# Streamed weights copied into contiguous blocks, with a ring of three double pieces in place of five single ones

## Chip, cores, metric

The kernel runs on one core of a Trainium2 chip. The metric is device microseconds of one execution. Each experiment was timed against the kernel before on the same chip, in turns. Medians are quoted, and ratios with 95% intervals.

## The reference, cut to what matters

Four residual layers, A, B, A, B, work on a sequence of 2048 rows of width 640. Layer A is recurrent. It cuts the sequence into segments, and the first 8 rows of the attention's input (the memory) come from the result of the segment before.

```python
for s in range(n_seg):
    xs = x[:, s * seg_len:(s + 1) * seg_len, :].copy()     # seg_len = 32
    h = jnp.concatenate([mem, xs], axis=1)                 # 8 + 32 rows of 640
    q = jnp.einsum('btd,dhe->bhte', h, Wq)                 # 32 heads of 192
    k = jnp.einsum('btd,dhe->bhte', h, Wk)
    v = jnp.einsum('btd,dhe->bhte', h, Wv)
    ...                                                    # masked softmax attention
    o = jnp.einsum('bhte,hed->btd', o, Wo)
    mem = o[:, :M, :].copy()                               # M = 8: needed by the next segment
    outs.append(o[:, M:, :])
```

The 64 segments of a layer A cannot run side by side, so a segment's latency is paid 64 times per layer and 128 times in all.

## The kernel before

Wk, Wq and Wv are each 640 x 6144 in bfloat16. They are viewed as 128 partitions x 5 row groups `b` x 6144 columns, and the columns are worked in four head groups `r` of 1536. Of the 60 pieces (3 weights, 4 `r`, 5 `b`) those with `b` of 0 to 2 stay in SBUF. The other 24 pieces, of 384 KB each, are streamed from DRAM again in every segment, through a ring of five. A piece has 3072 bytes per partition, and its rows are 61440 bytes apart in DRAM.

```python
def pieces(pool, m, r, nb=5):
    out = []
    for b in range(KC):
        if (m, r, b) in streamed:                      # b = 3, 4
            t = pool.tile([P, PW], BF16, name="wring", tag="wring", bufs=nb)
            nc.sync.dma_start(out=t[:], in_=wview[m][:, b, PW * r:PW * r + PW])
            out.append(t)
        else:
            out.append(res[m, r, b])
    return out
...
for s in range(NSEG):
    load_rows(xrs[s % 2], x_dram, s)                   # 4 small loads on SP's queue
    if s + 1 < NSEG:
        load_rows(hxs[(s + 1) % 2], xn_dram, s + 1)    # 4 more
    ...
    for r in range(NR):
        for m in "KQV":
            w = pieces(sp, m, r)
            for b in range(KC):
                for g in range(4):
                    nc.tensor.matmul(ps[32 * g:32 * g + 32, 0:384], lhsT=hT[:, b, :], rhs=rhs, ...)
            # K, Q: raw (ACT), then transposes to KT, QT (DVE); V: Vp (ACT, DVE)
        # scores S from KT and QT (PE); E = exp(S) (ACT); normalised to Pt; O = Pt Vp (PE); OT; W += OT Wo
    ...
    hT = hx_transpose(s + 1)                           # then its memory columns, from W: next segment
```

In the timelines below PE keeps to its queue's order: a matmul whose operand is not there holds what stands behind it.

The softmax here doesn't subtract the row's maximum and nothing guards it: scores larger than these inputs give would overflow.

Of the kernel before, what the change touches and what calls it, by code (L numbers as in the profile page):

```python
# [8 lines left out]
P = 128  # L9
BF16 = mybir.dt.bfloat16  # L10
# [88 lines left out]
class Kernel:  # L99
# [130 lines left out]
    def build_A_consts(self):  # L230
# [19 lines left out]
            nc.vector.memset(ones[32 * g:32 * g + 32, 32 * g:32 * g + 32], 1.0)  # L250
        self.ones_blk = ones

    def layer_A(self, x_dram, xn_dram, xout_dram, li):
        nc, tc = self.nc, self.tc
        KC, NSEG = self.KC, self.NSEG
        dram = self.dram
        NR = 4
        PW = 1536
        self.kqb_d = dram.tile([NSEG, P, NR, 224], BF16, name=f"kqb{li}")
        self.vb_d = dram.tile([NSEG * 8, NR, 4, 512], BF16, name=f"vb{li}")  # L260
        self.otb_d = dram.tile([NSEG, P, 384], BF16, name=f"otb{li}")
        wsrc = {"K": self.A_Wk, "Q": self.A_Wq, "V": self.A_Wv}
        wview = {m: w.rearrange("(p b) h d -> p b (h d)", b=KC) for m, w in wsrc.items()}
        streamed = {(m, r, b) for m in "KQV" for r in range(NR) for b in (3, 4)}
        with tc.tile_pool(name=f"A{li}_wres", bufs=1) as wres:
            res = {}
# [3 lines that stand above are left out]
                        if (m, r, b) not in streamed:  # L270
                            t = wres.tile([P, PW], BF16, name=f"w{m}{r}{b}")
                            nc.sync.dma_start(out=t[:], in_=wview[m][:, b, PW * r:PW * r + PW])
                            res[m, r, b] = t
            wo = wres.tile([P, 48, 640], BF16, name="wo_res")

            def pieces(pool, m, r, nb=5):
                out = []
                for b in range(KC):
                    if (m, r, b) in streamed:
                        t = pool.tile([P, PW], BF16, name="wring", tag="wring", bufs=nb)  # L280
                        nc.sync.dma_start(out=t[:], in_=wview[m][:, b, PW * r:PW * r + PW])
                        out.append(t)
                    else:
                        out.append(res[m, r, b])
                return out

            self.A_pre(xn_dram, li, pieces)
            for r in range(NR):
                nc.sync.dma_start(out=wo[:, 12 * r:12 * r + 12, :], in_=self.A_Wo.rearrange("h d m -> (h d) m").rearrange(
                    "(c p) m -> p c m", p=P)[:, 12 * r:12 * r + 12, :])  # L290
            self.A_chain(x_dram, xn_dram, xout_dram, li, pieces, wo)
            self.A_post(x_dram, xout_dram, li, wo)

    def A_pre(self, xn_dram, li, pieces):
        nc, tc, ev, KC, NSEG = self.nc, self.tc, self.ev, self.KC, self.NSEG
        NR = 4
        NT = NSEG // 16
        TP = P // NSEG
        with tc.tile_pool(name=f"A{li}_pre", bufs=1) as pp, \
                tc.tile_pool(name=f"A{li}_preps", bufs=8, space=bass.MemoryType.PSUM) as ps_:  # L300
            xv = xn_dram.rearrange("(s t) d -> t s d", t=32)
            xBT = pp.tile([P, KC, 8 * NSEG], BF16, name="xBT")
            for k in range(NT):
                xb = pp.tile([P, 640], BF16, name="xB", tag="xB", bufs=1)
                for t2 in range(TP):
                    nc.gpsimd.dma_start(out=xb[NSEG * t2:NSEG * t2 + NSEG, :], in_=xv[24 + TP * k + t2])
                pt = ps_.tile([P, 1024], BF16, name="pt", tag="bank")
                for b in range(KC):
                    self.transp(out=pt[:, P * b:P * b + P], in_=xb[:, :].rearrange("p (q b) -> p b q", b=KC)[:, b, :],
                                identity=self.ident[:, :])  # L310
                for t2 in range(TP):
                    t = TP * k + t2
                    ev.copy(out=xBT[:, :, :].rearrange("p b (s t) -> p b s t", t=8)[:, :, :, t],
                            in_=pt[:, 0:640].rearrange("p (b q) -> p b q", b=KC)[:, :, NSEG * t2:NSEG * t2 + NSEG])
            stage = [pp.tile([P, 16, 224], BF16, name=f"stage{i}") for i in range(2)]
            vst = [pp.tile([P, 4, 512], BF16, name=f"vst{i}") for i in range(1)]
            for t in stage:
                nc.vector.memset(t[:], 0.0)
            for t in vst:
                nc.vector.memset(t[:], 0.0)  # L320
            n = 0
            for r in range(NR):
                wk = pieces(pp, "K", r, 4)
                wq = pieces(pp, "Q", r, 4)
                for tb in range(NT):
                    st = stage[n % 2]
                    n += 1
                    for m, w in (("K", wk), ("Q", wq)):
                        for pi in range(4):
                            ps = ps_.tile([P, 512], F32, name="ps_pre", tag="bank")  # L330
                            for i in range(3):
                                c = 3 * pi + i
                                for b in range(KC):
                                    nc.tensor.matmul(ps[:, P * i:P * i + P], lhsT=w[b][:, P * c:P * c + P],  # L334
                                                     rhs=xBT[:, b, P * tb:P * tb + P], start=(b == 0), stop=(b == KC - 1))
                            src = ps[:, 0:384].rearrange("p (i s t) -> p i s t", i=3, t=8)
                            if m == "Q":
                                for i in range(3):
                                    o = 128 + 8 * (3 * pi + i)
                                    ev.copy(out=st[:, :, o:o + 8], in_=src[:, i])  # L340
                            else:
                                o = 32 * pi
                                ev.copy(out=st[:, :, o:o + 8], in_=src[:, 0])
                                ev.copy(out=st[0:64, :, o + 8:o + 16], in_=src[0:64, 1])
                                ev.copy(out=st[64:P, :, o + 16:o + 24], in_=src[64:P, 1])
                                ev.copy(out=st[:, :, o + 24:o + 32], in_=src[:, 2])
                    nc.gpsimd.dma_start(out=self.kqb_d[16 * tb:16 * tb + 16, :, r, :].rearrange("s p f -> p s f"), in_=st[:])
                wv = pieces(pp, "V", r, 4)
                for tb in range(NT):
                    vt = vst[0]  # L350
                    for g in range(4):
                        ps = ps_.tile([P, 512], F32, name="ps_pre", tag="bank")
                        for b in range(KC):
                            nc.tensor.matmul(ps[:, 0:384], lhsT=xBT[:, b, P * tb:P * tb + P], rhs=wv[b][:, 384 * g:384 * g + 384],
                                             start=(b == 0), stop=(b == KC - 1))
                        ev.copy(out=vt[:, g, 0:192], in_=ps[:, 0:192])
                        ev.copy(out=vt[:, g, 320:512], in_=ps[:, 192:384])
                    nc.gpsimd.dma_start(out=self.vb_d[P * tb:P * tb + P, r, :, :], in_=vt[:])

    def A_chain(self, x_dram, xn_dram, xout_dram, li, pieces, wo):  # L360
        nc, tc, KC, NSEG = self.nc, self.tc, self.KC, self.NSEG
        scale = float(self.Dh) ** -0.5
        NR = 4
        with tc.tile_pool(name=f"A{li}_ch", bufs=2) as sp, \
# [9 lines left out]
            def load_rows(dst, src, s):  # L374
                for g in range(4):
                    nc.sync.dma_start(out=dst[32 * g + 8:32 * g + 32, :], in_=src[32 * s:32 * s + 24, 160 * g:160 * g + 160])
# [11 lines left out]
            for s in range(NSEG):  # L388
                load_rows(xrs[s % 2], x_dram, s)
                if s + 1 < NSEG:  # L390
                    load_rows(hxs[(s + 1) % 2], xn_dram, s + 1)
                otb = sp.tile([P, NR, 12, 8], BF16, name="otb", tag="otb")
                kqb = vb = None
                W = pop.tile([P, 512], F32, name="ps_w", tag="w")
                for r in range(NR):
# [11 lines left out]
                    for m in "KQV":  # L407
                        w = pieces(sp, m, r)
# [9 lines left out]
                        if m == "V":  # L418
                            nc.scalar.activation(out=Vp[:, :].rearrange("p (a c) -> p a c", c=64)[:, 0:3, :],  # L419
                                                 in_=ps[:, 0:192].rearrange("p (a c) -> p a c", c=64), func=ACT.Copy)  # L420
# [71 lines left out]
                for g in range(4):  # L492
                    nc.gpsimd.dma_start(out=xout_dram[32 * s:32 * s + 24, 160 * g:160 * g + 160],  # L493
                                        in_=ob[32 * g + 8:32 * g + 32, :])
# [236 lines left out]
```

## Time and profile before

| | before |
|---|---|
| three runs: median, lowest, highest | 5964.28 us, 5961.47, 5976.45 |
| profiled span, clock granted to PE | 5972.0 us, 0.877 |
| the two recurrent chains | 2118.4 and 2125.4 us |
| mean segment | 34.22 us |
| SP's first load for the first layer norm | 55.2 us |

In the following a segment starts when the cast that completes its `hT` starts. A transfer has landed when the last of its 16 engines has reported. These numbers are worked out from the trace's records of transfers and instructions, as are all "per segment" numbers below. (The prediction's 34.07 us is the same mean over a shorter stretch.)

From the page of the kernel before, part 2: one digit for each fortieth of the span, in tenths. "PEclk" is the granted clock.

```profile
PE   1877777777777777767848777777777777777777
...
PEclk9988988988888888779979889888898888888898
DMA  5678888888888888830075888888888888887301
```

The two long plateaus, where DMA is at 8, are the two chains. PE shows 7 there: neither is saturated, so a chain of dependences decides.

From the page of before, part 3, DMA queues: number of packets, MB moved, and the time that the packets took as a share of 16 engines' span. Queue q1 carries SP's transfers, nearly all of them streamed weights.

```profile
q1 hardware_dynamic: 551376, 1319.70, 65.1%
```

From the page of before, part 4: the chain of work that ended last, as shares of the span by engine and by line.

```profile
DMA 41%; PE 37%; DVE 7%; issue 7%; ACT 5%; SPq 1%; POOL 1%; DVEq 0%; POOLq 0%; ACTq 0%
DMA wring<-in_A_Wv_dram 17%; PE ps_qkv L416 17%; DMA wring<-in_A_Wk_dram 12%; DMA wring<-in_A_Wq_dram 8%; PE ps_w L481 4%; ACT raw L424 2%; PE ps_num L539 2%; PE ps_pre L334 2%; PE ps_kv L539 2%; PE ps_bqk L539 1%; PE pp L516 1%; PE ps_o L467 1%; DMA kqb<-kqb 1%; PE ps_s L442 1%; DVE QT L426 1%
```

Streamed weights take 37% of the chain (17 + 12 + 8), and PE as much.

From the waits view of PE, before (what it waited for: us in total, number of waits, longest):

```profile
PE ps_qkv L416 <- DMA wring<-in_A_Wk_dram: 120.2, 180, 2.3
PE ps_qkv L416 <- DMA wring<-in_A_Wq_dram: 119.9, 215, 3.1
PE ps_qkv L416 <- DMA wring<-in_A_Wv_dram: 116.6, 240, 2.1
...
PE ps_w L481 <- issue: 45.0, 46, 2.4
...
PE ps_s L451 <- ACT E L450: 5.7, 26, 0.2
```

 "issue" marks a wait whose end the profile cannot explain; all such lines of this view come to 100 us.

From the timeline of SP, before, one segment's end (start, duration, engine, line, operation, count). One line can stand for several issues.

```profile
2005.47 2.21 SPq L281 DMA_DIRECT2D wring<-in_A_Wv_dram  x2
2007.73 1.92 SPq L376 DMA_DIRECT2D Xr<-in_A_x_dram  x4
2009.69 2.68 SPq L376 DMA_DIRECT2D Hx<-xn  x4
2012.50 0.83 SPq L281 DMA_DIRECT2D wring<-in_A_Wk_dram  x2
```

After V of `r` = 3, SP issues eight small row loads, and the next K stands behind them. On average V lands at 29.35 us and the last of the eight is issued at about the same moment, so the DMA queue runs empty. The gap between landings is some 2.9 us longer than usual. It is called the drain below.

From the timeline of before, one set of scores in the same chain:

```profile
2021.98 0.58 DVE L426 STREAM_TRANSPOSE QT<-raw 128x384 bf16<-128x384 bf16 x1 [1.35 <-ACT raw L424]
...
2022.62 0.25 PE L442 MATMUL ps_s<-QT,KT 128*32 128x40 bf16 x3
...
2023.16 0.22 PE L446 MATMUL ps_s<-QT,kqb 128*8 128x16 bf16 x4
...
2023.48 0.26 ACT L450 ACTIVATE E<-ps_s 128x112 bf16<-128x112 f32 x1 [1.52 <-PE ps_s L446]
```

### The profile page before, as it was taken

To read this page: it belongs to the slowest core of one execution; us is meant where nothing else is said; L and a number is where in the kernel's file an instruction comes from. 1 tells how busy PE (TensorE), PEld (TensorE's weight loads), DVE (VectorE), ACT (ScalarE), POOL (GpSimd) and SP (SyncE) were. 2 spreads that over 40 slices of the span, in tenths; PEclk is the share of its full clock that TensorE was granted. 3 is DMA by queue.
4 is the path that set the end of the run, shared out by engine and by line. 5 is a ranking of instruction groups with operands and counts; after the bars stand their busy time and mean duration, and the time that the engine had idled before them with its cause. 6 is when DMAs were issued, how large, how long until landed. Compare 5 with 4: busy or idle time off the path is not lost.

```text
span 5972.0 us, 227753 instructions
## 1 busy us (share of the span) xinstructions
PE 4427.1 (74%) x99706; PEld 2457.7 (41%) x99784; DVE 2244.9 (38%) x6994; ACT 1597.1 (27%) x4729; POOL 1529.6 (26%) x3332
## 2 busy tenths in 40 slices
PE   1877777777777777767848777777777777777777
PEld 1744444444444444333337344444444444444343
DVE  3333333333333333338444333333333333332383
ACT  1322222222222222224023222222222222222230
POOL 3122232322322322220011322322322322322100
PEclk9988988988888888779979889888898888888898
DMA  5678888888888888830075888888888888887301
GB/s 176 214 255 298 294 296 297 296 294 296 290 294 301 292 303 290 271 121 16 7 269 169 285 291 298 295 293 297 289 295 295 294 293 294 301 294 241 98 21 32
DMA packets 645399, 1470.22 MB, mean 246 GB/s; under 512 B 144160, under 2 KB 200448, under 8 KB 644400
## 3 DMA queue, kind: packets, MB, share of 16 engines
q1 hardware_dynamic: 551376, 1319.70, 65.1%
q0 software_dynamic: 91648, 135.06, 7.3%
q8 instruction: 780, 12.78, 0.8%
q14 instruction: 219, 1.79, 0.1%
q10 hardware_dynamic: 1376, 0.88, 0.1%
HBM read 1372.81 MB, written 82.35 MB: 244 GB/s over the span
## 4 chain that ended last, share of the span: by engine, by line
DMA 41%; PE 37%; DVE 7%; issue 7%; ACT 5%; SPq 1%; POOL 1%; DVEq 0%; POOLq 0%; ACTq 0%
DMA wring<-in_A_Wv_dram 17%; PE ps_qkv L416 17%; DMA wring<-in_A_Wk_dram 12%; DMA wring<-in_A_Wq_dram 8%; PE ps_w L481 4%; ACT raw L424 2%; PE ps_num L539 2%; PE ps_pre L334 2%; PE ps_kv L539 2%; PE ps_bqk L539 1%; PE pp L516 1%; PE ps_o L467 1%; DMA kqb<-kqb 1%; PE ps_s L442 1%; DVE QT L426 1%
## 5 line engine op out<-in xcount | busy, mean ns | idle before, releaser
L416 PE MATMUL ps_qkv<-wring,hT 128*32 128x384 bf16 x12288 | 1504.8, 364 | 389.5 <-DMA wring<-in_A_Wk_dram 120.2
L416 PEld LDWEIGHTS <-hT 128*32 128x32 bf16 x30720 | 959.3, 104 | 1419.4 <-issue 1054.3
L424 ACT ACTIVATE raw<-ps_qkv 128x384 bf16<-128x384 f32 x1024 | 501.9, 490 | 1742.6 <-PE ps_qkv L416 1698.4
L416 PE MATMUL ps_qkv<-wK,hT 128*32 128x384 bf16 x6144 | 707.6, 390 | 227.3 <-DVE hT L489 113.5
L416 PE MATMUL ps_qkv<-wQ,hT 128*32 128x384 bf16 x6144 | 756.8, 381 | 24.9 <-issue 17.5
L481 PE MATMUL ps_w<-wo_res,OT 128*32 128x160 bf16 x24576 | 628.3, 253 | 137.4 <-ACT OT L476 89.9
L401 POOL DMA_DIRECT2D vb<-vb x1024 | 571.3, 559 | 544.5 <-PE ps_qkv L416 231.4
L481 PEld LDWEIGHTS <-OT 128*32 128x32 bf16 x24576 | 495.7, 104 | 363.6 <-ACT OT L476 272.9
L431 DVE STREAM_TRANSPOSE KT<-raw 128x128 bf16<-128x128 bf16 x1024 | 258.5, 291 | 877.7 <-ACT raw L424 877.6
L406 POOL COPY QT<-kqb 128x96 bf16<-128x96 bf16 x512 | 135.9, 266 | 1638.2 <-PE ps_s L446 1537.8
L421 DVE CAST Vp<-ps_qkv 128x192 bf16<-128x192 f32 x512 | 183.1, 358 | 832.6 <-ACT Vp L419 832.6
L416 PE MATMUL ps_qkv<-wV,hT 128*32 128x384 bf16 x6144 | 430.9, 358 | 38.2 <-ACT raw L424 33.9
L426 DVE STREAM_TRANSPOSE QT<-raw 128x384 bf16<-128x384 bf16 x512 | 296.1, 578 | 403.4 <-ACT raw L424 397.1
L477 DVE CAST OT<-ps_o 128x240 bf16<-128x240 f32 x512 | 208.6, 407 | 575.0 <-ACT OT L476 575.0
L478 POOL COPY otb<-OT 128x96 bf16<-128x96 bf16 x512 | 139.0, 272 | 812.9 <-DVE OT L477 812.9
L476 ACT ACTIVATE OT<-ps_o 128x240 bf16<-128x240 f32 x512 | 189.5, 370 | 561.2 <-PE ps_o L471 553.7
L450 ACT ACTIVATE E<-ps_s 128x112 bf16<-128x112 f32 x512 | 134.7, 263 | 696.6 <-PE ps_s L446 696.6
L442 PE MATMUL ps_s<-QT,KT 128*32 128x40 bf16 x8192 | 206.7, 185 | 99.9 <-DVE QT L426 77.6
L493 POOL DMA_DIRECT2D xres<-ob x512 | 263.4, 523 | 50.1 <-DVE hT L489 43.9
L467 PEld LDWEIGHTS <-Vp 32*128 32x128 bf16 x8192 | 148.4, 92 | 243.2 <-issue 234.1
L442 PEld LDWEIGHTS <-KT 128*32 128x32 bf16 x8192 | 144.1, 94 | 250.0 <-DVE QT L426 228.5
L467 PE MATMUL ps_o<-Pt,Vp 32*128 32x40 bf16 x8192 | 192.0, 179 | 45.1 <-DVE Pt L460 45.0
(412 smaller groups left out, 6091.7 us busy)
## 6 DMA issues: line engine op xcount, KB each, us to landing
wring<-in_A_Wk_dram SPq DMA_DIRECT2D x1040, 384.0 KB
wring<-in_A_Wq_dram SPq DMA_DIRECT2D x1040, 384.0 KB
wring<-in_A_Wv_dram SPq DMA_DIRECT2D x1040, 384.0 KB
kqb<-stage POOLq DMA_DIRECT2D x32, 896.0 KB, 6.5
kqb<-kqb POOLq DMA_DIRECT2D x256, 112.0 KB, 5.0
vb<-vst POOLq DMA_DIRECT2D x32, 512.0 KB, 2.9
vb<-vb POOLq DMA_DIRECT2D x1024, 16.0 KB, 5.1
wo_res<-in_A_Wo_dram SPq DMA_DIRECT2D x8, 1920.0 KB
```

The lines of the kernel that those rows point to most:

```text
L401: nc.gpsimd.dma_start(out=vb[32 * g:32 * g + 8, :, :], in_=self.vb_d[8 * s:8 * s + 8, r:r + 2, g, :])
L416: nc.tensor.matmul(ps[32 * g:32 * g + 32, 0:384], lhsT=hT[:, b, :], rhs=rhs, start=(b == 0), stop=(b == KC - 1), tile_position=(0, 32 * g) ...
L424: nc.scalar.activation(out=raw[:], in_=ps[:, 0:384], func=ACT.Copy)
L426: nc.vector.transpose(out=QT[:, :, 8:40], in_=raw[:, :].rearrange("p (c j) -> p c j", j=32))
L431: nc.vector.transpose(out=kv[:, :, o, :], in_=rv[:, :, i, :])
L442: nc.tensor.matmul(S[32 * g:32 * g + 32, 40 * e:40 * e + 40], lhsT=KT[:, 4 * g + ks, :], rhs=QT[:, 3 * g + qc, :], start=False, stop=False ...
L467: nc.tensor.matmul(O[:, g, 40 * i:40 * i + 40], lhsT=Vp[32 * g:32 * g + 32, P * blk:P * blk + P], rhs=Pt[32 * g:32 * g + 32, 40 * e:40 * e ...
L476: nc.scalar.activation(out=ov[:, 0:2, :], in_=O[:, 0:2, 0:120], func=ACT.Copy)
L477: nc.vector.tensor_copy(out=ov[:, 2:4, :], in_=O[:, 2:4, 0:120])
L481: nc.tensor.matmul(W[32 * g:32 * g + 32, 0:160], lhsT=OT[:, c, 8:40], rhs=wo[:, 12 * r + c, 160 * g:160 * g + 160], start=(r == 0 and c == 0),
L493: nc.gpsimd.dma_start(out=xout_dram[32 * s:32 * s + 24, 160 * g:160 * g + 160], in_=ob[32 * g + 8:32 * g + 32, :])
L539: nc.tensor.matmul(ps[rows, n0:n0 + nn], lhsT=lhsT_fn(k), rhs=rhs_fn(k, n0, nn), **kw)
```

## The change

The intent: one transfer of 6144 bytes per partition instead of two of 3072, read from a block whose rows lie end to end, and a ring that holds six pieces instead of five. At the start twelve DRAM-to-DRAM copies lay the streamed weights out so. To make room, the tile `otb` goes from two buffers to one.

```diff
+        self.wst = {}
+        for r in range(4):
+            for m in "KQV":
+                t = self.dram.tile([P, 2, 1536], BF16, name=f"wst{m}{r}")
+                nc.sync.dma_start(out=t[:], in_=self.wview[m][:, 3:5, 1536 * r:1536 * r + 1536])
+                self.wst[m, r] = t
 ...
-            def pieces(pool, m, r, nb=5):
-                out = []
-                for b in range(KC):
-                    if (m, r, b) in streamed:
-                        t = pool.tile([P, PW], BF16, name="wring", tag="wring", bufs=nb)
-                        nc.sync.dma_start(out=t[:], in_=wview[m][:, b, PW * r:PW * r + PW])
-                        out.append(t)
-                    else:
-                        out.append(res[m, r, b])
+            def pieces(pool, m, r, nb=3):
+                t = pool.tile([P, 2, PW], BF16, name="wring", tag="wring", bufs=nb)
+                nc.sync.dma_start(out=t[:], in_=self.wst[m, r][:])
+                out = [res[m, r, b][:, :] for b in range(3)] + [t[:, 0, :], t[:, 1, :]]
                 return out
 ...    # the prologue before each chain: rings of 4 singles become rings of 2 doubles
-                otb = sp.tile([P, NR, 12, 8], BF16, name="otb", tag="otb")
+                otb = sp.tile([P, NR, 12, 8], BF16, name="otb", tag="otb", bufs=1)
```

More of the change, by code (lines that the diff above doesn't have):

```diff
@@ L251, in build_A_consts @@
         self.ones_blk = ones
+        wsrc = {"K": self.A_Wk, "Q": self.A_Wq, "V": self.A_Wv}
+        self.wview = {m: w.rearrange("(p b) h d -> p b (h d)", b=self.KC) for m, w in wsrc.items()}
+        self.wst = {}
[4 more added lines that the diff above has]
+                self.wst[m, r] = t
     def layer_A(self, x_dram, xn_dram, xout_dram, li):
@@ L261, in layer_A @@
         self.otb_d = dram.tile([NSEG, P, 384], BF16, name=f"otb{li}")
-        wsrc = {"K": self.A_Wk, "Q": self.A_Wq, "V": self.A_Wv}
-        wview = {m: w.rearrange("(p b) h d -> p b (h d)", b=KC) for m, w in wsrc.items()}
+        wview = self.wview
         streamed = {(m, r, b) for m in "KQV" for r in range(NR) for b in (3, 4)}
@@ L322, in A_pre @@
             for r in range(NR):
-                wk = pieces(pp, "K", r, 4)
-                wq = pieces(pp, "Q", r, 4)
+                wk = pieces(pp, "K", r, 2)
+                wq = pieces(pp, "Q", r, 2)
                 for tb in range(NT):
@@ L347, in A_pre @@
                     nc.gpsimd.dma_start(out=self.kqb_d[16 * tb:16 * tb + 16, :, r, :].rearrange("s p f -> p s f"), in_=st[:])
-                wv = pieces(pp, "V", r, 4)
+                wv = pieces(pp, "V", r, 2)
                 for tb in range(NT):
```

## The prediction

> **What bounds the kernel now.** The two recurrent layers take most of the span: 128 segments of 34.07 us mean (spacing of the hT casts in the trace, 0.7 to 2.3 ms). A segment streams 24 pieces of 384 KB. In the slices view DMA is 88% busy at about 295 GB/s; the chain of waits gives 37% of the span to the streamed weights, 37% to PE. In the waits view PE waits for streamed pieces 357 us in all, 2.8 us per segment: the most that streaming alone can give back directly.
>
> Issue and landing of every piece, timed against the segment's start, show three regimes:
> - At 29.2 us the last piece (V, r=3) lands. Only then is the last of eight small row loads issued (29.3 us), then the next K (29.8 us), which lands at 33.4 us: 4.2 us between landings instead of 1.25, a drain of about 2.9 us.
> - At 10 to 14 us piece 12 is issued late (11.0 us; its predecessor lands at 13.7): the DMA share dips from 0.97 to 0.72, since PE still held the slot. The ring of five is too short here.
> - After 14 us pieces land back to back, 1.25 us apart, and PE waits.
>
> **Costs.**
> Packets: one of 3072 bytes takes 121 ns at the median, 142 in the mean; 4096 bytes take 160, 5120 take 196. The slope is about 26.8 bytes per ns, the fixed part about 7 ns. So 6144 bytes should take about 235 ns rather than 2x121. That agrees in direction with the Trainium skill, "DMA: Bandwidth & Descriptors", "Why small descriptors are slow" (a fixed cost per packet); at 3 KB it is a 3% matter. The stalls (142 against 121) look proportional to bytes in other reads too (1280 bytes: 66 against 55; 768: 42 against 36), so I expect contiguity not to remove them: about 276 ns in the mean. With half the semaphore packets: an estimated 0.8 us per segment.
>
> Ring: three doubles are six pieces, one more ahead. Where PE holds the slots (10 to 14 us) DMA gets up to one piece, 1.25 us, further ahead, but a slot comes free only when both halves are used: 0.8 us.
>
> Unchanged: the drain (the eight small loads still follow V of r=3, and the last still waits for it, as the instruction order shows), PE's work, the 4.8 us from V's landing to the next hT.
>
> Added: twelve DRAM-to-DRAM copies, 9.4 MB, at the head of SP's queue, before the setup on the chain (SP does short setup copies until 55 us). At about 300 GB/s an estimated 30 us, once, nearly all exposed.
>
> **Sum.** 128 x 1.6 = 205 us less, 30 more: 5964 - 175 = about 5790 us. Range 5650 to 5880; faster by over 2% 0.67, within 2% 0.29, slower 0.04.
>
> **What would show it.** Packets of 6144 bytes near 235 ns median, 276 mean; 2.4 us between landings of doubles; segments near 32.5 us; a shallower dip at 10 to 14 us; the drain still about 3 us; PE's wait for streamed weights well below 357 us; the first ln_x load some 30 us later than 55 us.
>
> **What would make it wrong.** Contiguous blocks ending the stalls (mean near 240 ns): far faster, PE-bound, near 5600. Or transfers cut into smaller packets, or blocks whose rows collide in memory: no gain. Or PE, blocked in order on a whole double, delaying the scores behind it: the ring's gain lost, within 2%.

## More of the kernel before

The order of instructions on each engine is fixed by a scheduler when the kernel is built, and it need not be the order of the source.

Times inside a segment are means over both chains: 124 segments, or 110 in the table of landings.

PE waits 356.7 us for streamed pieces, and hardly at all (5.7 us) for the exponentials E of the scores.

The score matmuls follow the transposed Q (QT) at once and run through in about 0.75 us; E follows. No matmul on a streamed piece of V stands between them.

## The result, and the profile after

| | before | after |
|---|---|---|
| median of four runs (lowest, highest) | 5968.23 us (5961.47, 5976.45) | 5948.58 us (5945.19, 5965.11) |
| ratio, 95% interval | | 0.9972 [0.9949, 0.9995] |
| profiled span, clock | 5972.0 us, 0.877 | 5963.0 us, 0.876 |
| chains | 2118.4, 2125.4 us | 2095.7, 2105.6 us |
| mean segment | 34.22 us | 33.88 us |
| start of the first `hT` cast of the first chain | 377.49 us | 409.34 us |

A ratio is the mean time of one kernel's fast runs over that of the other's fast runs of the same rounds, so it is not quite the ratio of the medians quoted. Below, a ratio is turned into microseconds as (ratio - 1) x 5966; here that is -17 us. The change was predicted at -175 us.

From the page of after, part 2, the slices:

```profile
PE   0777777777777777767848677777777777777778
...
PEclk9989888888988888879879888888888888888898
DMA  5668888888888888840065788888888888887201
```

From part 3 of that page, the queue of the streamed weights; it has fewer packets, as intended, and a smaller share:

```profile
q1 hardware_dynamic: 330000, 1329.03, 63.0%
```

From part 4 of that page, the chain:

```profile
PE 40%; DMA 31%; issue 11%; DVE 9%; ACT 8%; POOL 1%; SPq 1%; DVEq 0%; ACTq 0%; POOLq 0%
PE ps_qkv L419 17%; DMA wring<-wstV 14%; DMA wring<-wstQ 10%; PE ps_w L484 7%; DMA wring<-wstK 3%; ACT raw L427 2%; DVE QT L429 2%; PE ps_num L542 2%; PE ps_bqk L542 2%; PE ps_kv L542 2%; ACT Vp L422 1%; PE ps_s L445 1%; PE pp L519 1%; PE ps_o L470 1%; ACT OT L479 1%
```

The streamed weights' part of the chain fell from 37% to 27%. "issue", DVE and ACT took it over: 7 + 7 + 5 became 11 + 9 + 8.

From the waits view of PE, after:

```profile
PE ps_s L454 <- ACT E L453: 143.6, 361, 0.6
...
PE ps_qkv L419 <- DMA wring<-wstQ: 73.3, 140, 1.6
PE ps_qkv L419 <- DMA wring<-wstK: 69.6, 88, 2.3
...
PE ps_w L484 <- issue: 64.6, 57, 2.7
...
PE ps_qkv L419 <- DMA wring<-wstV: 63.4, 112, 1.7
```

PE waits 206.3 us for streamed pieces, 150 us less. Yet the wait for E rose from 5.7 to 143.6 us, and the "issue" lines from 100 to 187 us in all. Some of those last up to 3.2 us, as long as waits for weights, so 206 us is the least that weights can still cost here. The wait changed its name more than it went away.

From the timeline of after, one set of scores:

```profile
2017.34 0.18 PE L445 MATMUL ps_s<-QT,KT 128*32 128x40 bf16 x1
...
2017.55 0.51 PE L419 MATMUL ps_qkv<-wring,hT 128*32 128x384 bf16 x8
...
2017.87 0.17 PE L449 MATMUL ps_s<-QT,kqb 128*8 128x16 bf16 x1
...
2017.92 0.18 PE L449 MATMUL ps_s<-QT,kqb 128*8 128x16 bf16 x3
...
2018.33 0.26 ACT L453 ACTIVATE E<-ps_s 128x112 bf16<-128x112 f32 x1
...
2018.64 0.20 PE L454 MATMUL ps_s<-E,ones_blk 128*128 128x80 bf16 x1 [0.21 <-ACT E L453]
```

Here the eight matmuls on V's double piece (L419) stand in PE's queue ahead of the last score matmuls. They cannot start before the whole double has landed, and E cannot start before them. Per segment, in us from its start:

| | V(r=2) lands | E(r=2) starts | K(r=3)'s evacuation starts | V(r=3) lands | next hT | E's start after QT's start, r = 0..3 |
|---|---|---|---|---|---|---|
| before | 21.99 | 21.86 | 25.14 | 29.35 | 34.22 | 1.23, 1.16, 1.36, 1.26 |
| after | 20.94 | 22.06 | 24.66 | 27.98 | 33.88 | 1.13, 2.05, 2.30, 1.99 |

V(r=2) lands 1.05 us earlier, but E of `r` = 2 starts 0.20 us later. And V(r=3) lands 1.37 us earlier, but the next segment starts only 0.34 us earlier.

From the timeline of SP, after, at the start:

```profile
0.75 0.70 SPq L259 DMA_DIRECT2D wstK<-in_A_Wk_dram  x1
...
18.49 2.13 SPq L259 DMA_DIRECT2D wstV<-in_A_Wv_dram  x1
20.95 4.84 SPq L187 DMA_DIRECT2D wbd<-zeros_t  x3
...
85.25 1.31 SPq L208 DMA_DIRECT2D ln_x<-in_A_x_dram  x3
```

From the same view of before:

```profile
1.34 1.34 SPq L187 DMA_DIRECT2D wbd<-zeros_t  x3
...
55.19 30.44 SPq L208 DMA_DIRECT2D ln_x<-in_A_x_dram  x16
```

In after the twelve copies stand ahead of the same setup. They delay the first layer norm's loads by 30.1 us (85.25 - 55.19), and the first `hT` cast by 31.9 us.

Packets of the streamed weights, over both chains: 3072 bytes took 121 ns at the median and 142.0 in the mean before; 6144 bytes take 234 and 273.0 after. The prediction had 235 and 276. So the packets do what was predicted and the segment does not.

### The profile page after: what moved, and what is told of

Read it like the earlier page. It is cut to its first block, busy times and chain, and to the rows that moved or that the text cites. A ratio compares the mean times of both kernels' runs of the same rounds, so it can differ in the third digit from the quotient of the medians.

```text
span 5963.0 us, 224613 instructions
## 1 busy us (share of the span) xinstructions
PE 4281.2 (72%) x99784; PEld 2571.8 (43%) x99784; DVE 2232.8 (37%) x6994; ACT 1587.3 (27%) x4729; POOL 1537.5 (26%) x3332
## 4 chain that ended last, share of the span: by engine, by line
PE 40%; DMA 31%; issue 11%; DVE 9%; ACT 8%; POOL 1%; SPq 1%; DVEq 0%; ACTq 0%; POOLq 0%
PE ps_qkv L419 17%; DMA wring<-wstV 14%; DMA wring<-wstQ 10%; PE ps_w L484 7%; DMA wring<-wstK 3%; ACT raw L427 2%; DVE QT L429 2%; PE ps_num L542 2%; PE ps_bqk L542 2%; PE ps_kv L542 2%; ACT Vp L422 1%; PE ps_s L445 1%; PE pp L519 1%; PE ps_o L470 1%; ACT OT L479 1%
## 5 line engine op out<-in xcount | busy, mean ns | idle before, releaser
L419 PEld LDWEIGHTS <-hT 128*32 128x32 bf16 x30720 | 933.9, 105 | 1115.9 <-issue 765.6
L419 PE MATMUL ps_qkv<-wring,hT 128*32 128x384 bf16 x12288 | 1025.0, 363 | 226.9 <-DMA wring<-wstQ 73.3
L484 PE MATMUL ps_w<-wo_res,OT 128*32 128x160 bf16 x24576 | 654.9, 262 | 162.5 <-ACT OT L479 75.6
L419 PE MATMUL ps_qkv<-wK,hT 128*32 128x384 bf16 x6144 | 571.6, 384 | 210.4 <-DVE hT L492 98.3
L419 PE MATMUL ps_qkv<-wQ,hT 128*32 128x384 bf16 x6144 | 658.0, 387 | 28.1 <-issue 16.8
L484 PEld LDWEIGHTS <-OT 128*32 128x32 bf16 x24576 | 515.4, 108 | 327.7 <-ACT OT L479 223.6
L419 PE MATMUL ps_qkv<-wV,hT 128*32 128x384 bf16 x6144 | 428.3, 367 | 17.0 <-issue 14.9
L422 ACT ACTIVATE Vp<-ps_qkv 128x192 bf16<-128x192 f32 x512 | 169.5, 331 | 781.0 <-PE ps_s L449 729.5
L445 PE MATMUL ps_s<-QT,KT 128*32 128x40 bf16 x8192 | 221.0, 184 | 166.2 <-DVE QT L429 104.1
L470 PE MATMUL ps_o<-Pt,Vp 32*128 32x40 bf16 x8192 | 221.5, 180 | 97.4 <-DVE Pt L463 97.0
L470 PEld LDWEIGHTS <-Vp 32*128 32x128 bf16 x8192 | 195.6, 93 | 215.0 <-issue 206.5
```

The costliest lines, as they stand in the source:

```text
L422: nc.scalar.activation(out=Vp[:, :].rearrange("p (a c) -> p a c", c=64)[:, 0:3, :], in_=ps[:, 0:192].rearrange("p (a c) -> p a c", c=64), ...
L445: nc.tensor.matmul(S[32 * g:32 * g + 32, 40 * e:40 * e + 40], lhsT=KT[:, 4 * g + ks, :], rhs=QT[:, 3 * g + qc, :], start=False, stop=False ...
L470: nc.tensor.matmul(O[:, g, 40 * i:40 * i + 40], lhsT=Vp[32 * g:32 * g + 32, P * blk:P * blk + P], rhs=Pt[32 * g:32 * g + 32, 40 * e:40 * e ...
L484: nc.tensor.matmul(W[32 * g:32 * g + 32, 0:160], lhsT=OT[:, c, 8:40], rhs=wo[:, 12 * r + c, 160 * g:160 * g + 160], start=(r == 0 and c == 0),
```

## The experiments

Eighteen runs were made, in five calls, each call on one chip; four of them repeat a kernel. All gave correct results. What was expected of each is printed with it, and several expectations were missed: e_direct and e_best came out faster than any range given, e_block5 slower; e_dirv and e_rows fell where their second theory had put them; e_same and e_pitchv lie between two theories; e_direct2 was 35 us faster than the change, not 60 to 90. Four theories were at stake:

- *Held scores*: doubling the piece made the scheduler put the scores behind V's matmuls; this new wait took back the gain.
- *Layout*: rows end to end in DRAM are worse to read than rows far apart, whatever the packets.
- *Copies*: the scratch in DRAM is itself slower to read than the weights' own place.
- *Depth*: the ring's sixth piece alone is worth little (rival), or about what was predicted.

Where a statement is about layout alone, the order of PE's instructions was compared and found identical to the change's: e_direct, e_same, e_pitch, e_pad, e_p12, e_p24. In other runs the scheduler moved more than was asked. The matmuls on resident pieces of Q that start before those on the streamed K of `r` = 1, 2 and 3 number, in each of eleven segments counted, 13, 25, 37 before, in e_ring6 and in e_block5; 17, 33, 45 in the change and in the six kernels named; 17, 27, 39 in e_vlate, e_dirv and e_pitchv; 13, 25, 36 in e_bv; 12, 24, 36 in e_rows and e_best.

### First call: order, depth, layout, each by itself

**e_vlate**: the change, with V's eight streamed matmuls and the evacuation of V put after the scores. An ordering edge without a semaphore holds the scheduler to it. The same edit is called "scores first" below.

```diff
-                        for b in range(KC):
+                        for b in range(3 if m == "V" else KC):
 ...    # after the last score matmul:
+                    for b in (3, 4):
+                        for g in range(4):
+                            mm = nc.tensor.matmul(psV[32 * g:32 * g + 32, 0:384], lhsT=hT[:, b, :],
+                                                  rhs=wV[b][:, 384 * g:384 * g + 384], start=False, stop=(b == KC - 1), ...)
+                            tc.add_manual_dep(mm.ins, last.ins.name, ..., reason="scores first")
```

> The changed kernel with one thing more: the eight V matmuls that need the streamed double are issued behind the score matmuls of the same r, not between them. Theory H (V's double now lands 1.46 us earlier in the segment, but PE, which issues in order, holds the last scores behind V's double, so the exponential of r=1 to 3 starts 2.0 to 2.3 us after the last Q transpose instead of 1.15 to 1.35 as before): that distance goes back to about 1.25 us, segments fall from 33.7 to about 32.9 us, time about 5840 us (5780 to 5890). Rival R (PE's own work or the drain at the end of a segment sets the pace, whatever the order): segments stay at 33.7, time within 15 us of 5949.

Measured: 5860.65 us, 0.9817 [0.9791, 0.9843], -109 us. E follows QT by 1.14, 1.33, 1.43 and 1.26 us again, and a segment takes 33.12 us. In the waits view of PE for this kernel the large wait for E is gone; what is left is for weights:

```profile
PE ps_qkv L419 <- DMA wring<-wstK: 90.5, 115, 1.9
PE ps_qkv L419 <- DMA wring<-wstQ: 77.7, 144, 2.3
...
PE ps_qkv L452 <- DMA wring<-wstV: 44.7, 78, 1.7
```

So the held scores are a real wait, and the edit that takes it away gains 92 us over the change (the scheduler also moved matmuls on Q, as told above). That alone does not show that the change *brought* the loss; e_bv below is the control.

**e_ring6**: the kernel before with a ring of six singles; no doubles, no copies. PE's order is that of before.

```diff
-            def pieces(pool, m, r, nb=5):
+            def pieces(pool, m, r, nb=6):
-                otb = sp.tile([P, NR, 12, 8], BF16, name="otb", tag="otb")
+                otb = sp.tile([P, NR, 12, 8], BF16, name="otb", tag="otb", bufs=1)
```

> The kernel before with a ring of six single pieces instead of five (otb with one buffer, as in the change); no copies, no doubles; PE's order is that of before. Theory H: the extra piece of depth is worth 0.8 us per segment where the scores are not held: segments 33.1 to 33.4 us, time about 5870 us (5830 to 5900). Rival R: depth is worth nothing, 5964 +- 15. Rival D (the whole small gain of the change came from the larger packets): also 5964.

Measured: 5874.90 us, 0.9841 [0.9819, 0.9863], -95 us, 33.47 us per segment. The sixth piece was predicted at 0.8 x 128 = 102 us. The size of the depth term holds, and these two short edits alone gain more than the whole change. The single `otb` buffer was not tested alone. The clock granted to PE was 0.867 to 0.871 in all four runs, against 0.874 to 0.883 for the kernel before in the same rounds; why, and what e_ring6 would take at the same clock, was not looked into.

**e_direct**: the change without its copies; the doubles are read straight from the weights, as two rows of 3072 bytes per partition.

```diff
-                nc.sync.dma_start(out=t[:], in_=self.wst[m, r][:])
+                nc.sync.dma_start(out=t[:], in_=wview[m][:, 3:5, PW * r:PW * r + PW])
```

> The changed kernel with its doubles loaded straight from the weights (two rows of 3072 bytes per partition in one transfer), without the copies; PE's order is exactly that of the change. It gives up the 6144-byte packets (0.8 us of DMA time per segment) and saves the 31 us at the start. Theory H: the landing of V is only partly what sets the segment, so segments rise by 0.3 to 0.8 us over the change's 33.7: time 5955 to 6020. If packets and contiguity are worth nothing: segments 33.7, 5918 +- 15.

Measured: 5873.11 us, 0.9847 [0.9823, 0.9871], -91 us, 33.41 us per segment. E follows QT by 1.13, 1.91, 2.28 and 1.94 us, as late as in the change, and PE waits for E as long. From the waits view of PE, e_direct:

```profile
PE ps_s L448 <- ACT E L447: 142.8, 356, 0.6
```

Yet the gain of e_ring6 is kept. So doubles with held scores took no longer than six singles here (at a granted clock of 0.881 to 0.883, so what the doubles cost at one clock is not known), and what is lost against this run comes in with the copies. The change stood at -17 us in its own runs, 74 us behind: 30 of them are the start, and the other 44 would lie in reading from the blocks.

**e_block5**: the kernel before with its 24 pieces copied to contiguous blocks of 384 KB. Ring and order are of before.

```diff
+                t = self.dram.tile([P, 1536], BF16, name=f"wst{m}{r}{b}")
+                nc.sync.dma_start(out=t[:], in_=self.wview[m][:, b, 1536 * r:1536 * r + 1536])
```

> The kernel before, with its single 3 KB pieces copied once into contiguous 384 KB blocks: contiguity alone, with the ring of five and the order of before. My reckoning: packets of 3072 bytes stay at 121 ns median and about 142 mean, segments 34.1 us, the start 30 to 35 us later: 5995 us (5980 to 6010). If contiguity ends stalls: mean under 130 ns and time under 5940.

Measured: 6031.09 us, 1.0101 [1.0078, 1.0124], +60 us: 30 for the copies and 30 from reading, though the packets have the same size and mean time (141.3 against 142.0 ns). A segment takes 34.52 us instead of 34.22. Contiguity costs time here without larger packets too.

### Second call: which part of the layout

**e_same** keeps the change, but the scratch has the weights' own layout, so the packets are of 3072 bytes. **e_pitch** has rows of 6144 bytes, one packet each, 61440 bytes apart.

```diff
 # e_same
+        full = {m: self.dram.tile([P, 5, 6144], BF16, name=f"wst{m}") for m in "KQV"}
-                t = self.dram.tile([P, 2, 1536], BF16, name=f"wst{m}{r}")
+                t = full[m][:, 3:5, 1536 * r:1536 * r + 1536]
 # e_pitch
+        full = {m: self.dram.tile([P, 10, 2, 1536], BF16, name=f"wst{m}") for m in "KQV"}
-                t = self.dram.tile([P, 2, 1536], BF16, name=f"wst{m}{r}")
+                t = full[m][:, r]
```

> The changed kernel, same order on PE, with the copies made into a scratch of the weights' own layout (rows of 3072 bytes, 12288 apart, 61440 per partition): the copies and the scratch stay, the contiguous blocks and the 6144-byte packets go. Theory L (the layout of the blocks makes the slowest engine of a transfer later): segments 33.4 us as with the doubles straight from the weights, 31 us lost at the start: about 5904 us (5890 to 5920). Theory S (it is the scratch memory, wherever its rows lie, that reads more slowly than the input): segments 33.9, about 5949 us.

> The changed kernel, same order on PE, with each 6144-byte row of a block 61440 bytes after the last one, as the weights' partitions are, rather than end to end: the 6144-byte packets stay, the contiguity goes. Theory P (rows end to end make the engines collide): spread from the first to the last engine of a transfer back from 1.9 to about 1.75 us, segments 33.2 to 33.4 us, about 5885 us (5865 to 5905). Theory K (the large packet itself does it, a slow packet being twice as long): segments 33.9 us, about 5949 us.

Measured: e_same 5933.52 us, 0.9927 [0.9910, 0.9944], -44 us, 33.66 us per segment; e_pitch 5902.28 us, 0.9874 [0.9856, 0.9893], -75 us, 33.42 us per segment. From the windows view of e_same, 700 to 2200 us (window, length, then busy time of PE, PE's weight loads, DVE, ACT and POOL with instruction counts, granted clock, DMA share, GB/s):

```profile
700.00:2200.00 1500.00, 1106.74 (x31661) 663.20 (x31653) 519.25 (x1782) 415.49 (x1246) 456.77 (x1026) 0.89 0.88 300
```

The same view of e_pitch:

```profile
700.00:2200.00 1500.00, 1107.95 (x31858) 665.63 (x31848) 522.18 (x1791) 417.59 (x1253) 460.08 (x1033) 0.89 0.86 301
```

Three things follow. No cost of the copies beyond their 30 us shows: without these 30 us e_same would stand at -74, between the two runs of e_direct (-91 and, later, -64), which differ in chip. The larger packets are worth 31 us, with an interval of some 15 either way, or 0.24 us per segment. And the DMA share falls while the rate hardly rises. Over both chains the packets took 29.70 us of 16 engines' time per segment with e_same and 28.84 with e_pitch. Of the 0.86 us of DMA time saved, 0.24 came off the segment and 0.62 became idle DMA. In the change itself one such idle stretch lies some 3 us into the segment: K of `r` = 1 is issued only 2.4 us after the segment's start, in the median segment and in nearly every one, when its slot comes free, and the DMA share is 0.51 between 3.0 and 3.5 us.

**e_dirv**: e_direct with scores first.

```diff
 # e_direct, and the edit of e_vlate
```

> Both repairs together: doubles straight from the weights (no copies) and V's streamed matmuls behind the scores. If the two gains are independent (the first run's 0.76 us per segment for the order, the second's 76 us for doing without the staged blocks): about 5780 us (5755 to 5805), segments near 32.65 us. If they draw on the same slack: 5830 to 5860.

Measured: 5843.37 us, 0.9780 [0.9760, 0.9799], -131 us. Scores first also helps without the copies, by 40 us against e_direct's ratio in the first call.

**e_rows**: e_dirv, with the eight row loads on the GpSimd queue.

```diff
             def load_rows(dst, src, s):
                 for g in range(4):
-                    nc.sync.dma_start(out=dst[32 * g + 8:32 * g + 32, :], in_=...)
+                    nc.gpsimd.dma_start(out=dst[32 * g + 8:32 * g + 32, :], in_=...)
```

> The double repair with one more thing: the eight small row loads of a segment are issued on GpSimd's queue, so that the next K no longer waits behind them for the landing of V. The drain of DMA by about 2.9 us per segment should go. Where DMA still sets the pace, segments fall by 1 to 2 us more: about 5600 us (5530 to 5700). If PE's chain sets the pace by now, or GpSimd's eight further issues (0.5 us each) delay the K and V of the past that PE needs: 5780 or slower.

Measured: 5798.41 us, 0.9702 [0.9681, 0.9723], -178 us: 47 us better than e_dirv on the same chip. The drain is gone: K of `r` = 0 lands 2.7 us after V of `r` = 3, against 5.2 in e_dirv. But the scheduler also put the matmuls on streamed K earlier in PE's queue (12, 24, 36 in the count above, instead of 17, 27, 39), so the 47 us belong to both together. The Trainium skill ("DMA: Bandwidth & Descriptors", "Rules for kernel authors") says that spreading transfers over the issuing engines does not help bandwidth and only saves issue time. Here it took a wait out of an in-order queue, which is another thing than bandwidth. From the waits view of PE, first e_dirv, then e_rows, where the largest wait for weights is now for K:

```profile
PE ps_qkv L413 <- DMA wring<-in_A_Wk_dram: 93.4, 119, 2.5
...
PE ps_qkv L413 <- DMA wring<-in_A_Wk_dram: 219.5, 293, 3.4
```

### Third call: controls, and the best of both

**e_bv**: the kernel before with scores first, the control for e_vlate.

```diff
 # before, and the edit of e_vlate
```

> The kernel before (five single pieces, no copies) with the same reordering as in the first run: both streamed pieces of V behind the scores. A control for it. Theory H (the change's own order is what holds the scores; before held them by one piece at most, exponential 1.15 to 1.35 us after the last Q transpose): little to gain, 5945 to 5985 us. Rival G (scores first is simply a better order, worth 90 us to any version): about 5880 us.

Measured: 5892.33 us, 0.9870 [0.9853, 0.9888], -78 us. This is nearly the 92 us that the same edit gained in the change. The difference of 14 us is inside the two intervals together (some 23 us). So the held scores, though they are there to be seen, do not explain where the expected gain went: the theory of held scores falls as the main cause, and e_direct, with the same wait for E and without the loss, says the same. With scores first in both kernels the change is worth 109 - 78 = 31 us.

**e_pad**: the change with rows 6656 bytes apart instead of 6144.

```diff
-                t = self.dram.tile([P, 2, 1536], BF16, name=f"wst{m}{r}")
+                full = self.dram.tile([P, 3328], BF16, name=f"wst{m}{r}")
+                t = full[:, 0:3072].rearrange("p (b f) -> p b f", b=2)
```

> The changed kernel, same order on PE, with its rows of 6144 bytes 6656 bytes apart instead of end to end. Theory P1 (an exact lockstep of the engines' addresses[...]): the small step of 512 bytes breaks it, spread from first to last engine back to about 1.75 us, about 5900 us as with the wide pitch. Theory P2 (it is that the whole transfer lies within a short stretch of memory, whatever the exact step): spread 1.9 us, about 5950 us.

Measured: 5947.73 us, 0.9971 [0.9954, 0.9988], -17 us, as the change. A small pad does not help.

**e_pitchv**: e_pitch with scores first.

```diff
 # e_pitch, and the edit of e_vlate
```

> Wide pitch (rows of 6144 bytes, 61440 apart) and V's streamed matmuls behind the scores; to be set against the first run (same order, rows end to end, ratio 0.982 to before) and against the wide pitch in the change's order (0.987). If the cost of rows end to end reaches the time only through the held scores: about the same as the first run, 5860 us (5845 to 5875). If it is paid in any order: 50 us faster, about 5805 us.

Measured: 5823.32 us, 0.9761 [0.9745, 0.9778], -143 us, 34 us better than e_vlate's ratio (another chip). The layout is paid for with scores first too.

**e_best**: six singles straight from the weights, scores first, row loads on the GpSimd queue.

```diff
 # e_ring6, and the edits of e_vlate and e_rows; no copies
```

> No staging: six single pieces of 3 KB, V's streamed matmuls behind the scores, the small row loads on GpSimd's queue. Against the same with three doubles (5798 us): if releasing a slot by halves is worth something, 5740 to 5790 us; if not, 5800 us.

Measured: 5692.49 us, 0.9539 [0.9524, 0.9555], -275 us, 31.97 us per segment. It beats both kernels. From the waits view of PE for it:

```profile
PE ps_qkv L416 <- DMA wring<-in_A_Wk_dram: 77.5, 143, 1.9
```

Against e_rows its source differs only in six singles for three doubles, and K's wait fell from 219.5 to 77.5 us. The two ran on different chips and PE's order is not quite the same; that freeing slots by halves is the reason is likely, but was not separated.

### Fourth and fifth call: how far apart must the rows be

The prediction was wrong and the layout's cost was still open. **e_p12** and **e_p24** are e_pad with 6144 and 12288 elements per row: rows 12288 and 24576 bytes apart. **e_after2** is the change again, and **e_direct2** is e_direct again.

```diff
-                full = self.dram.tile([P, 3328], BF16, name=f"wst{m}{r}")
+                full = self.dram.tile([P, 6144], BF16, name=f"wst{m}{r}")     # e_p12; e_p24: 12288
```

> The changed kernel, same order on PE, rows of 6144 bytes 12288 bytes apart (a transfer covers 1.5 MB instead of 0.75). Theory P2 (the cost belongs to a dense stretch and goes as it widens): between the change and the wide pitch, 5910 to 5945 us. If only the very wide pitch helps: 5950 us, spread 1.9 us.

> As the last, 24576 bytes apart (3 MB). Theory P2: 5900 to 5925 us, spread from first to last engine near 1.75 us. If a multiple of 8192 in the pitch is itself harmful[...]: slower than the change, over 5965 us.

> The changed kernel itself, to have it in the same rounds as the next: 5950 us (5935 to 5965).

> The doubles straight from the weights, without staging, once more, in the same rounds as the change: 5875 us, 75 us (60 to 90) less than the change; of these 31 us at the start and the rest, 0.35 us per segment, in the chain. If the chains take the same time, 31 us less only.

Measured: e_p12 5921.94 us, 0.9927 [0.9904, 0.9949], -44 us; e_p24 5928.22 us, 0.9929 [0.9910, 0.9947], -42 us; e_after2 5939.24 us, 0.9947 [0.9932, 0.9963], -32 us; e_direct2 5904.06 us, 0.9892 [0.9872, 0.9911], -64 us. On this chip e_direct gains 27 us less than on the first, which is the size of difference between chips that any comparison across calls must allow. The differences between e_after2 and the wider pitches, 10 to 12 us, are within the intervals.

**e_pitch2** and **e_after3**, e_pitch and the change unaltered, were then run on one chip.

```diff
 # the kernels e_pitch and after, unaltered
```

> The wide pitch again (rows of 6144 bytes, 61440 apart), in the same rounds as the change. If rows end to end cost time: 35 to 60 us less than the change, segments 0.3 to 0.45 us shorter, spread from first to last engine 1.73 against 1.9 us. If that was the chip's: within 15 us of the change.

> The changed kernel in the same rounds: 5935 to 5955 us, segments 33.8 us, spread 1.9 us.

Measured: e_pitch2 5891.88 us, 0.9865 [0.9838, 0.9891], -81 us; e_after3 5941.62 us, 0.9959 [0.9933, 0.9985], -24 us. The two have the same instructions in the same order on PE, packets of the same size and the same copies; only the distance of the rows in DRAM differs. It is worth 56 us (0.0094 x 5966), with some 22 either way. Layout is shown as a cause.

How it acts is not shown. The packets are not slower: 274.7 ns in the mean with the wide pitch, 271.2 end to end. But a transfer is spread over 16 engines and counts as landed with the last. The Trainium skill ("DMA: Bandwidth & Descriptors", "Why a DMA increments its semaphore by 16 and not by 1") says that each engine adds one when its own data has landed and only the full 16 mean that all is there; the trace has these 16 updates for each transfer. Their spread, first to last, in the mean over all transfers of both chains:

| rows | pieces of 768 KB, us | pieces of 384 KB, us |
|---|---|---|
| 61440 bytes apart | 1.73 (e_pitch), 1.77 (e_pitch2), 1.76 (e_same), 1.75 (e_direct), 1.91 (e_rows) | 1.76 (before), 1.92 (e_ring6), 1.87 (e_best) |
| 24576 apart | 1.83 (e_p24) | |
| 12288 apart | 1.89 (e_p12) | |
| 6656 apart | 1.94 (e_pad) | |
| end to end | 1.92 (after), 1.92 (e_after2), 1.95 (e_after3) | 1.90 (e_block5) |

Among kernels that differ in layout alone, closer rows go with a later last engine, and the DMA engines are idle 5.17 us per segment in e_after3 against 4.60 in e_pitch2. That fits a last engine that keeps the others waiting. But e_ring6, e_rows and e_best have rows 61440 bytes apart, the same wide spread, and are among the fastest kernels here. So the spread does not come from layout alone, and a wide spread does not by itself cost time: that it carries the 56 us is not shown. What in the memory makes some engines late is open too: the trace gives no addresses.

## Why the prediction was right or wrong

**The depth term was right in size, not shown in its reason.** "a slot comes free only when both halves are used: 0.8 us", 102 us in all; e_ring6 measured 95. With doubles, which the term was about, e_direct gave 91 on the same chip and 64 on another. The reason given was a dip at 10 to 14 us that one more piece would fill. It was not filled: the mean DMA share from 10 to 14 us was 0.86 before and 0.87 in e_ring6, and the DMA engines stayed idle 4.25 and 4.30 us per segment. What fell in e_ring6 was the mean packet, from 142.0 to 138.4 ns, or 0.7 us per segment at 192 packets for each engine; whether depth brings that is open. The match in size is in part luck.

**The start was right.** An estimated 30 us; the first load came 30.1 us later.

**The packets were right, and the step from them to the time was wrong.** This is the step that failed: "I expect contiguity not to remove them: about 276 ns in the mean. With half the semaphore packets: an estimated 0.8 us per segment". It made two assumptions.

1. A nanosecond of DMA time saved is a nanosecond off the segment. The saving was there, 0.86 us of DMA time per segment from e_same to e_pitch, but 0.24 us (31 us per run, not 102) came off the segment; the rest became idle DMA.
2. Contiguous rows are neutral except for packet size. They cost 56 us against rows far apart (e_pitch2 and e_after3), and 30 us with singles (e_block5): about 0.2 to 0.4 us per segment. The mean packet time does not show it, and how the layout costs time stays open.

So the term stands at -31 + 56 = +25 us instead of -102: 127 us, most of the 158 us between the predicted -175 and the measured -17.

**The account adds up.** In us per run, each step from two runs that differ in it, or from the timeline:

| step | predicted | measured | from |
|---|---|---|---|
| ring of six pieces | -102 | -95 | e_ring6 |
| doubles for singles | 0 | +17 (+4, +31) | e_direct, e_direct2 against e_ring6 |
| copies at the start | +30 | +30 | timeline of SP |
| scratch itself | 0 | +4 | e_same less 30, against the mean of the e_direct runs |
| packets of 6144 bytes | -102 | -31 | e_same to e_pitch |
| rows end to end | in the line above | +56 | e_pitch2 to e_after3 |
| sum (the predicted one is -174 before rounding) | -175 | -19 | the change: -17, -32, -24 |

The steps were taken on several chips, and one and the same kernel differed by 27 us between two of them. So the small terms (doubles, scratch) cannot be told from 0. Nor is the sum an independent check: neighbouring steps share a run, which cancels, and what is left is e_pitch (-75) and the 56 us between e_pitch2 and e_after3. It does say that these agree across chips with the change itself.

**"Unchanged: ... the 4.8 us from V's landing to the next hT" was wrong.** It was 4.87 us before and 5.90 after, and 5.78 in e_ring6 as well. When the weights come earlier, V of `r` = 3 is no longer all that the segment's end waits for. From the evacuation of K of `r` = 3 to the next `hT` all kernels with the original order need much the same: 9.08 us before, 9.22 after, 9.09 in e_ring6, 9.18 in e_direct; and that evacuation, after the held scores of `r` = 2, came only 0.48 us earlier than before. A landing brought forward by 1.37 us thus gave 0.34.

**The third warning came true in the trace, but not in the account.** "PE, blocked in order on a whole double, delaying the scores behind it": E came up to 1 us later. Without the control e_bv it would have passed for the cause, since undoing it gained 92 us. But the same edit gained 78 in the kernel before, where no double exists. Why it helps there was not settled. The second warning, "blocks whose rows collide in memory: no gain", named the right place; whether they collide, the trace cannot say.

**The rest.** Doubles landed 2.35 us apart in the segment's last third (predicted 2.4). The drain stayed. The dip at 10 to 14 us did not get shallower (mean DMA share 0.86 before, 0.85 after; lowest half microsecond 0.72 and 0.75). PE's wait for weights, as far as the view names it, fell as predicted, from 357 to 206 us, and other waits took its place.

## What to carry to other kernels

A saving in a transfer's packet time is worth only what its landing gains, and what depends on that landing: find out which wait ends last once the first saving has been made, before adding the second. When an edit to the new kernel "wins back" the loss, make the same edit to the old kernel before calling it the cause. Try the ring's depth, the issue queue and the instruction order, each a few lines, before laying data out anew: here these three together gave 4.6%, and the whole change 0.3%.

## What the Trainium skill lacked or had wrong

- "DMA: Bandwidth & Descriptors", "Latency and other measured facts": the row on the HBM row pitch advises to pad the pitch by a few KiB or to lay tiles out contiguously; it is about pitches of 512 KiB and more. Here, where the pitch was 61440 bytes, contiguous rows of 6144 bytes were 56 us slower in a run of 5.9 ms than the wide pitch, and a pad of 512 bytes gave nothing (0.9971 against 0.9972 for the change). The page has nothing on pitches of this size.
- The same page, "Why a DMA increments its semaphore by 16 and not by 1": it says that the engines finish independently, but not by how much. Here the last was 1.73 to 1.95 us behind the first, in the mean. Where layout alone was changed the spread followed it, but it was as wide (1.92) in e_ring6, whose rows are far apart.
- The same page, "Why small descriptors are slow": a fixed cost per packet. The trace agrees, with 2 x 121 - 234 = 8 ns, 3%, for one packet saved out of two of 3072 bytes; the page's own sum (bytes / 32 + 3 cycles) gives an estimated 3% at this size too. What the page does not have is what such a saving is worth: 0.24 us came off a segment of 34 us.
- The same page, "Rules for kernel authors": spreading transfers over the issuing queues only saves issue time. It lacks the case that the queue's head waits for an earlier landing: moving eight small loads away ended a drain of some 2.5 us per segment and gained 47 us, together with the change in PE's order that came with it (e_dirv to e_rows). The rule to use 1 MiB or more per transfer for the greatest bandwidth was not tested; below it, 768 KB per transfer took as long as 384 KB (e_direct 0.9847, e_ring6 0.9841).
